# One core, column-normalised attention into a soft mixture of experts: first unit in one load, eight products of ones, 23 slots, half of turned v on VectorE, a new order

## Chip, cores and metric

One core of one Trainium2 chip. The metric is device time in microseconds (us). Before the change three runs took 286.63, 289.55 and 290.04 us, median 289.55 us.

## What is computed

B, N, C = 4, 5056, 256. All arrays are float32.

```
qn = q / (norm(q, axis=1) + 1e-6);  kn likewise          # norms over N, one per column
a  = softmax(kn.T @ qn / tau, axis=-1)                   # per batch, 256 x 256
x  = (v @ a).reshape(20224, 256)
logits = x @ phi                                         # 20224 x 32
d  = softmax(logits, axis=0);  slots = d.T @ x           # 8 experts x 4 slots x 256
out_e = relu(slots_e @ w1_e) @ w2_e                      # 256 -> 1024 -> 256
y  = softmax(logits, axis=1) @ out                       # 20224 x 256
```

q, k and v are read once (62 MB), v a second time in turned form for some of its parts (12.6 MB), the weights once (16.8 MB); 20.97 MB are written.

## The kernel before

**Stages.** q and k come in 40 units (ten per batch, 1 MB each: 128 partitions with 8 KB in a row; every unit has up to four tiles of 128 rows). For every tile TensorE adds kT q into one PSUM bank (`score`): straight from fp32 (L329, 4 instructions) or from a high and a low part (L335, 6 instructions), which ScalarE (`cast`, L274) and GpSimd (`low`, L278) make. ScalarE squares the unit (L289) and VectorE adds the squares (L307). After ten units the batch's norms, softmax and the product with phi follow (`att_...`), which give M, 256 x 32. v comes in 20 parts p (five per batch, 1 MB). The logits are M against v turned; for parts 2 to 13 the turned v is loaded (`load_vt`), for 0, 1 and 14 to 19 TensorE turns it (`turn`, L472, four 128 x 128 blocks into a bank) and ScalarE copies the bank to SBUF (`turned`, L477, 32 copies). `gather` (L601) then sums weighted v into slots. After the last part come the expert products (`up` L745, `relu`, `flip_h`, `back_h`, `down` L778, `o_copy`, `o_fold`, `o_back`) and the output (`out_mul` L816, `out_evict` L833, `store`), 40 blocks of softmax weights against the slots. The softmax over 32 slots (`c_max`, `c_sub`, `c_exp`, `c_sum`, `c_rec`, `c_mul`, `c_flip`) works on `nat`, 128 x 1280 per batch, mostly in VectorE passes.

**Order.** Nothing is scheduled by the compiler. `plan` lists some 1200 steps; `run` (L160) issues them in the sequence of the list `ORDER`, and every engine works through its own share of that sequence in order. All DMAs are issued by SyncE's queue (SP) in that order too: if one has to wait for its buffer, all behind it wait.

**Buffers.** All big tiles live in 22 slots of 8 KB per partition, named by `SLOTS`; a tile is written once the last reader of its slot's former tile is done. PSUM's eight banks are named by `BANKS` in the same way. The four `nat` tiles (5 KB each) and later the turned weights `cT` have places of their own.

**Start.** Unit 0 comes in three loads (L859: tile 0, tile 1, tiles 2 and 3). `constants` (identity, ones, an Exp to load ScalarE's table) stands behind the first products and squares. `wake` (L238) exists, but `WAKES` is empty.

Of the kernel before, what the change touches and what calls it, by code (L numbers as in the profile page):

```python
# [8 lines left out]
F32 = mybir.dt.float32  # L9
# [19 lines left out]
DVE_TURNED = set()  # L29

SAME = set()
WAKES = ()
# [62 lines left out]
]  # L95
SLOTS = {
# [70 lines left out]
def colnorm_attention_soft_moe(  # L167
# [22 lines left out]

    def slot(name, shape, dt=F32):
        return large.tile(shape, dt, tag=f"s{SLOTS[name]}", name=name)

    def bank(name):
        return ps.tile([P, 512], F32, tag=f"b{BANKS[name]}", name=name)

# [659 lines left out]
    for u in range(NU):  # L856
        b, i = divmod(u, UB)
        if u == 0:
            for lo, hi in ((0, 1), (1, 2), (2, 4)):  # L859
                at(-3, load_qk, 0, lo, hi)  # L860
# [204 lines left out]
```

## Time and profile before

| | |
|---|---|
| median of the runs | 289.55 us |
| the profiled execution | 288.49 us, its span 286.6 us |
| TensorE matmul, weight load busy | 250.2, 206.1 us |
| ScalarE, VectorE, GpSimd busy | 211.5, 200.7, 142.1 us |
| DMA | 112.90 MB, 394 GB/s over the span, queue share 96.7% |

The span is what the profiler saw of one execution from its first to its last event; the execution's own time is 1.9 us more. A share of busy time is a mean over stages: in the first 230 us all is read, in the last 55 us all is written, and GpSimd has work in the first 180 us only. A queue share near 100% means that bytes are moving nearly always.

### The profile page before, as it was taken

The numbers are of one execution on the slowest core, as the hardware profiler recorded it, in microseconds if no ns is written. First come the engines' busy times: TensorE is split into PE (matmuls) and PEld (weight loads), VectorE is DVE, ScalarE is ACT, GpSimd is POOL, SyncE is SP. The second block draws the span as 40 slices with busy tenths as digits, with TensorE's granted clock in tenths as the row PEclk, the third lists the DMA queues.
The fourth block names the chain that finished last, engine by engine and source line by source line (L and its number), as shares of the span: only waits on it lengthen the run. The fifth ranks groups of instructions, "written<-read, shape, count | busy, mean of one in ns | idle before, by whom it ended". The sixth has DMA issues, their size and how long they took to land.

```text
span 286.6 us, 6411 instructions
## 1 busy us (share of the span) xinstructions
PE 250.2 (87%) x2542; PEld 206.1 (72%) x2542; DVE 200.7 (70%) x386; ACT 211.5 (74%) x341; POOL 142.1 (50%) x118
## 2 busy tenths in 40 slices
PE   5799989999899998999999999999989899697300
PEld 3589879998699896787879779876643787595200
DVE  0156998778767679799579899589772487977600
ACT  3699999989989998989998978786633257446300
POOL 0379899798996998398899395100000000000000
PEclk9999999999999999999999999999989999959855
DMA  7999999999999999999999999999999959999996
GB/s 217 413 428 418 374 383 416 404 419 420 421 421 345 389 413 389 352 420 422 414 370 365 423 423 420 423 418 420 416 417 425 399 238 384 420 415 408 414 423 256
DMA packets 16301, 112.90 MB, mean 394 GB/s; under 512 B 1936, under 2 KB 1936, under 8 KB 3472
## 3 DMA queue, kind: packets, MB, share of 16 engines
q1 hardware_dynamic: 16272, 112.50, 96.7%
q8 instruction: 20, 0.33, 0.5%
q14 instruction: 9, 0.07, 0.1%
HBM read 91.52 MB, written 20.97 MB: 392 GB/s over the span
## 4 chain that ended last, share of the span: by engine, by line
PE 55%; DMA 23%; DVE 9%; ACT 4%; issue 2%; SPq 1%; DVEq 0%; ACTq 0%
PE S L335 19%; DMA v<-in_v_dram 10%; PE S L329 10%; DMA raw<-in_qk_dram 10%; PE op_None L816 4%; PE G L601 4%; DVE o L833 4%; PE T L472 3%; PE H L745 3%; PE O L778 3%; DMA x<-in_vt_dram 2%; DVE A L307 2%; PE L L492 2%; PE op L816 2%; PE Mp L425 1%
## 5 line engine op out<-in xcount | busy, mean ns | idle before, releaser
L278 POOL TENSOR_TENSOR hl<-raw,hl 128x512 fp32r<-128x512 f32 x108 | 137.5, 1312 | 33.5 <-ACT hl L274 27.0
L307 DVE TENSOR_TENSOR A<-sq,A 128x512 f32<-128x512 f32 (+1 forms) x144 | 95.2, 688 | 20.8 <-ACT sq L289 18.9
L335 PE MATMUL S<-hl 128*128 128x256 f32 x648 | 94.8, 295 | 0.0
L335 PEld LDWEIGHTS S<-hl 128*128 128x128 f32 x648 | 83.3, 190 | 3.9 <-issue 2.3
L289 ACT ACTIVATE sq<-raw 128x2048 f32<-128x2048 f32 (+2 forms) x40 | 71.5, 1803 | 6.5 <-DMA raw<-in_qk_dram 4.0
L329 PE MATMUL S<-raw 128*128 128x256 f32 (+1 forms) x208 | 52.2, 396 | 8.1 <-DMA raw<-in_qk_dram 8.1
L274 ACT CAST hl<-raw 128x1024 fp32r<-128x1024 f32 (+1 forms) x69 | 56.3, 863 | 3.1 <-DMA raw<-in_qk_dram 3.1
L329 PEld LDWEIGHTS S<-raw 128*128 128x128 f32 (+1 forms) x208 | 36.3, 195 | 15.5 <-DMA raw<-in_qk_dram 10.7
L816 PE MATMUL op_None<-so,cT 32*128 32x256 f32 x240 | 22.3, 436 | 3.4 <-DVE cT L720 2.7
L833 DVE COPY o<-op_None 128x512 f32<-128x512 f32 x30 | 18.9, 681 | 7.1 <-PE op_None L816 5.7
L833 ACT COPY o<-op_None 128x512 f32<-128x512 f32 x30 | 15.9, 591 | 9.2 <-PE op_None L816 9.1
L816 PEld LDWEIGHTS op_None<-so,cT 32*128 32x128 f32 x240 | 17.0, 204 | 7.7 <-DVE cT L720 3.5
L492 PE MATMUL L<-x,M 128*32 128x256 f32 (+1 forms) x320 | 20.6, 379 | 0.6 <-DMA x<-in_vt_dram 0.6
L601 PE MATMUL G<-v,dn 128*32 128x256 f32 x312 | 19.8, 381 | 1.3 <-DMA v<-in_v_dram 1.3
L477 ACT COPY x<-T 128x512 f32<-128x512 f32 x32 | 17.6, 602 | 2.3 <-PE T L472 2.3
L472 PE MATMUL T<-ident,v 128*128 128x128 f32 x124 | 16.8, 274 | 1.0 <-DMA v<-in_v_dram 0.9
L601 PEld LDWEIGHTS G<-v,dn 128*32 128x32 f32 x312 | 10.4, 109 | 7.3 <-DMA v<-in_v_dram 2.1
L472 PEld LDWEIGHTS T<-ident,v 128*128 128x128 f32 x124 | 14.0, 142 | 2.0 <-issue 0.8
L492 PEld LDWEIGHTS L<-x,M 128*32 128x32 f32 x320 | 10.3, 109 | 6.7 <-DVE cs L700 1.0
L816 PE MATMUL op<-so,cT 32*128 32x128 f32 x160 | 11.1, 324 | 2.8 <-ACT o L833 1.5
L816 PEld LDWEIGHTS op<-so,cT 32*128 32x128 f32 x160 | 9.3, 205 | 4.4 <-ACT o L833 1.9
L833 ACT COPY oh<-op 128x256 f32<-128x256 f32 x20 | 6.4, 381 | 6.8 <-PE op L816 6.7
(115 smaller groups left out, 247.8 us busy)
## 6 DMA issues: line engine op xcount, KB each, us to landing
raw<-in_qk_dram SPq DMA_DIRECT2D x37, 1024.0 KB, 8.9
v<-in_v_dram SPq DMA_DIRECT2D x16, 1024.0 KB, 9.3
w<-in_moe_w_dram SPq DMA_DIRECT2D x16, 1024.0 KB, 19.6
out_dram<-o SPq DMA_DIRECT2D x15, 1024.0 KB, 9.2
x<-in_vt_dram SPq DMA_DIRECT2D x12, 1024.0 KB, 7.8
out_dram<-oh SPq DMA_DIRECT2D x4, 1024.0 KB, 6.4
v<-in_v_dram SPq DMA_DIRECT2D x4, 896.0 KB, 10.3
raw<-in_qk_dram SPq DMA_DIRECT2D x2, 768.0 KB, 8.3
```

What stands on the lines that cost most here:

```text
L274: act.copy(parts(u, lo, hi)[:, :, 0::2, :], raws[u][:, lo:hi])
L278: pool.tensor_tensor(hl[:, :, 1::2, :], raws[u][:, lo:hi], hl[:, :, 0::2, :].bitcast(F32), op=ALU.subtract)
L289: act.activation(sqs[u][:, n : NT[u]], raws[u][:, n : NT[u]], AF.Square)
L307: dve.tensor_tensor(a[r], s[r, j], a[r], op=ALU.add)
L329: pe.matmul(sm, raw[r, j, 1, cols], raw[r, j, 0, :], start=first, stop=False, skip_group_check=True)
L335: pe.matmul(sm, hl[:, w, cols], hl[:, y, :], start=first, stop=False, skip_group_check=True)
L472: pe.transpose(tp[:, P * jj : P * jj + P], vtile(p, 4 * h + jj)[:, P * m : P * m + P], ident)
L477: to(xt(p)[:, m, h * UT : h * UT + UT], tps[p, h, m])
L492: pe.matmul(L[S * g : S * g + S, :n, :], M[:, m, :], x[:, :n, S * g : S * g + S], start=m == 0 and g not in void, stop=m == 1, skip_group_ ...
L601: pe.matmul(gp[S * g : S * g + S, :C], dn[:, x, j, :], vtile(p, j), start=x == 0 and j < G, stop=x == n - 1 and j >= G,)
L816: pe.matmul(ops[b, p, hf, g][:, h, :], cT[b][r, 4 * i : 4 * i + 4, :].rearrange("s j t -> s (j t)"), rhs[r], start=True, stop=True,)
L833: (dve.tensor_copy if g % 2 else act.copy)(dst, ops[b, p, hf, g])
```

## The change

- Unit 0 comes in one load (0 to 4).
- `WAKES = ((-8, 8),)`: eight products of `ones` by `ones` (128 x 128) ahead of all scores. `constants` moves to the front of every engine's list.
- `DVE_TURNED` names (p, h, 1) for all 20 parts: of the 32 copies of turned v, the 16 with m = 1 go to VectorE.
- 23 slots (0 to 22). The room comes from `nat`: only `nat0` and `nat1` keep places of their own, `nat2` and `nat3` take a slot each when their batch's first logits are ready; `cT3` takes the place of `nat2`.
- `ORDER`, `SLOTS` and `BANKS` are new throughout.

The diff without the three lists:

```
-DVE_TURNED = set()
+DVE_TURNED = {(9, 1, 1), (16, 0, 1), (10, 1, 1), (4, 0, 1), ...}
-WAKES = ()
+WAKES = ((-8, 8),)
+    def short(name):
+        t = slot(name, [P, 2 * C, 4]).rearrange("p c x -> p (c x)")
+        return t[:, : 8 * PB * S].rearrange("p (j s) -> p j s", s=S)
-    nat = [keep.tile([P, 8 * PB, S], F32, tag=f"nat{b}", name=f"nat{b}") for b in range(B)]
+    nat = [keep.tile([P, 8 * PB, S], F32, tag=f"nat{b}", name=f"nat{b}") for b in range(2)] + [None, None]
     def logit_nat(p):
         b, q = divmod(p, PB)
+        if nat[b] is None:
+            nat[b] = short(f"nat{b}")
     def c_flip(b, p):
         if b not in cT:
             if b == 0:
-                cT[b] = slot("cT0", [P, 2 * C, 4]).rearrange("p c x -> p (c x)")[:, : 8 * PB * S].rearrange(
-                    "p (j s) -> p j s", s=S
-                )
+                cT[b] = short("cT0")
+            elif b == 3:
+                cT[b] = nat[b - 1]
-            for lo, hi in ((0, 1), (1, 2), (2, 4)):
-                at(-3, load_qk, 0, lo, hi)
+            at(-3, load_qk, 0, 0, 4)
```

The new lists as the DMA queue sees them (q: unit of q and k, v: part of v, t: turned part, a: w1, b: w2, s: store of batch and part), before and after:

```
q0 q0 q0 q2 q4 q3 q1 q6 q5 q8 q7 q9 q10 q13 q11 q12 few v0 q14 q16 q15 q20 t3 v1 q19 t2 vh q17 t4 q21 q18 q23
q27 q26 q22 q25 v6 q24 v2 q35 q28 v3 t6 v4 q29 t5 q32 t7 q33 q30 q31 q34 t9 t8 q36 v9 q37 v5 v7 t10 v8 q38 t11
t12 q39 t13 v17 v14 v16 v15 v18 v12 v19 v10 v11 a1 v13 a3 a5 b01 a7 a6 a4 a2 a0 b00 b03 b02 b11 b10 b13 b12
s04.0 s01.0 s03.0 s10 s11 s14 s04.1 s20 s13 s12 s03.1 s24 s01.1 s32 s33 s30 s21 s31 s23 s34 s22

q0 q5 q6 q1 q3 q4 q9 q2 q7 q10 q8 q15 q11 q14 q12 v0 q13 q17 q16 v1 q19 q18 few t3 t2 q23 t4 q22 q20 q21 q37
q27 q24 q28 q29 q26 v2 q25 q31 t5 v4 vh t7 t6 q34 q30 t8 v3 t9 q32 q33 v6 v14 q35 q38 v5 t10 q36 t11 t13 v7
t12 v8 v9 q39 v16 v15 v17 v19 a1 a3 v18 v11 b00 v10 v12 v13 a0 a5 a2 a4 a7 a6 b03 b01 b02 b10 b11 b13 b12
s01.0 s03.0 s04.0 s11 s14 s12 s10 s01.1 s20 s03.1 s24 s13 s22 s32 s31 s30 s23 s04.1 s34 s33 s21
```

Other places that the prediction speaks of. In the old order ScalarE has `c_exp(2)` between the last part's exponentials and the sums that follow them (`tally`); in the new one it stands behind `last_back`, right ahead of `relu`. In the new order VectorE's `c_max(2)`, `c_sub(2)`, `c_mul(1)` and six of the `c_flip` steps of batches 0 and 1 stand behind `last_back` instead of ahead of it. Behind `o_copy(0)` VectorE's new list goes: `c_max(3)`, two `c_flip`, four copies of batch 0's first two output blocks, store.

## Rows read from the trace of the kernel before

**Rows 1.** Busy time by stretch (the window in us and its length, then busy time and instructions of PE, PEld, DVE, ACT and POOL, the granted TensorE clock, the DMA share, GB/s).

```profile
0.00:8.00 8.00, 3.78 (x8) 2.52 (x8) 0.00 (x0) 2.44 (x3) 0.20 (x4) 1.00 0.72 226
8.00:20.00 12.00, 10.58 (x54) 8.77 (x55) 5.09 (x18) 10.16 (x9) 5.96 (x7) 1.00 1.01 427
20.00:160.00 140.00, 135.62 (x1160) 119.30 (x1163) 111.23 (x200) 131.28 (x176) 121.28 (x97) 1.00 0.99 398
160.00:184.00 24.00, 23.14 (x230) 19.75 (x223) 22.98 (x43) 20.15 (x39) 14.61 (x11) 1.00 1.01 421
184.00:212.00 28.00, 27.13 (x364) 19.25 (x368) 19.61 (x50) 19.44 (x57) 0.00 (x0) 1.00 1.01 419
212.00:228.00 16.00, 15.07 (x214) 7.95 (x207) 7.41 (x11) 4.30 (x9) 0.00 (x0) 0.89 1.01 420
228.00:240.00 12.00, 11.26 (x271) 10.16 (x273) 8.65 (x21) 6.61 (x18) 0.00 (x0) 1.00 0.71 285
240.00:286.60 46.60, 23.64 (x266) 18.39 (x259) 25.69 (x46) 17.08 (x37) 0.00 (x0) 0.75 0.95 391
```

**Rows 2.** What the DMA queue's issues waited for between 20 and 160 us (total us, times, longest).

```profile
SPq L252 <- PE S L335: 24.8, 11, 4.6
SPq L467 <- PE S L335: 24.2, 7, 5.7
SPq L448 <- PE S L335: 11.3, 5, 3.5
SPq L252 <- ACT sq L289: 9.0, 3, 4.7
```

**Rows 3.** Pieces of the chain that ended last, in order of time (start, length, what; x counts instructions): the loads and products of the scores, of turned v, the last v load and the last stages.

```profile
13.41 1.99 PE S L329 x8
15.40 1.43 PE S L335 x12
...
20.23 0.86 PE S L329 x4
...
37.33 7.05 DMA v<-in_v_dram
...
47.95 0.44 PE T L472 x4
...
184.02 2.37 PE T L472 x20
...
188.27 1.73 PE G L601 x32
...
199.80 0.86 PE L L492 x16
...
207.64 1.17 ACT nat L696
...
211.88 8.74 PE H L745 x64
...
221.39 1.60 PE hTp L763 x12
223.00 3.67 PE O L778 x128
...
227.89 3.02 PE op L816 x61
```

**Rows 4.** TensorE's first instructions in order of time (start, busy time, what, count, idle before).

```profile
3.50 3.78 PE L329 MATMUL S<-raw 128*128 128x256 f32 x8 [3.50 <-DMA raw<-in_qk_dram]
8.43 1.99 PE L329 MATMUL S<-raw 128*128 128x256 f32 x8 [1.14 <-DMA raw<-in_qk_dram]
10.92 1.99 PE L329 MATMUL S<-raw 128*128 128x256 f32 x8 [0.50 <-DMA raw<-in_qk_dram]
```

**Rows 5.** The DMA queue's issues in order of time: the first loads and the first stores.

```profile
0.74 7.99 SPq L252 DMA_DIRECT2D raw<-in_qk_dram  x11
...
231.60 0.35 SPq L842 DMA_DIRECT2D out_dram<-oh  x1
```

**Rows 6.** The copies out of PSUM and VectorE's passes over `nat` (line, engine, operation, tiles, count, busy us, mean ns).

```profile
L477 ACT COPY x<-T 128x512 f32<-128x512 f32 x32 | 17.6, 602 | 2.3 <-PE T L472 2.3
L833 DVE COPY o<-op_None 128x512 f32<-128x512 f32 x30 | 18.9, 681 | 7.1 <-PE op_None L816 5.7 <-issue 1.4
L693 DVE TENSOR_TENSOR nat<-nat,cm 128x1280 f32<-128x1280 f32 x4 | 5.9, 1476 | 0.0
L720 DVE STREAM_TRANSPOSE cT<-nat 128x256 f32<-128x256 f32 x20 | 8.1, 424 | 0.2
```

More of the change, by code (lines that the diff above doesn't have):

```diff
@@ L28 @@
 LT = {2, 3, 4, 5, 6, 7, 8, 9, 10, 11, 12, 13}
-DVE_TURNED = set()
+DVE_TURNED = {(9, 1, 1), (16, 0, 1), (10, 1, 1), (4, 0, 1), (5, 0, 1), (11, 1, 1), (17, 1, 1), (15, 0, 1), (18, 0, 1), (0, 0, 1), (12, 0, 1), (1, 0, 1), (7, 1, 1), (13, 1, 1), (19, 1, 1), (2, 0, 1), (8, 0, 1), (14, 0, 1), (6, 1, 1), (3, 1, 1), (9, 0, 1), (15, 1, 1), (10, 0, 1), (16, 1, 1), (4, 1, 1), (11, 0, 1), (5, 1, 1), (6, 0, 1), (18, 1, 1), (0, 1, 1), (12, 1, 1), (2, 1, 1), (17, 0, 1), (7, 0, 1), (19, 0, 1), (8, 1, 1), (14, 1, 1), (3, 0, 1), (1, 1, 1), (13, 0, 1)}
 SAME = set()
-WAKES = ()
+WAKES = ((-8, 8),)
 ORDER = [
[59 rows of a table removed]
[59 rows of a table added]
 ]
 SLOTS = {
[25 rows of a table removed]
[25 rows of a table added]
 }
 BANKS = {
[33 rows of a table removed]
[33 rows of a table added]
 }
```

234 rows, old and new, of tables (BANKS, ORDER, SLOTS) are left out of this document.

## The prediction

> **What bounds the kernel now.** I read the busy time by stretch first. From 8 to 20 us and from 160 to 228 us bytes flow at 419 to 427 GB/s; I take 424 as the full stream. Three stretches fall short: the first 8 us, 20 to 160 us (398) and 228 to 240 us (285), where the loads are done and the stores have not begun [rows 1]. The waits of the DMA queue say why the middle is short: between 20 and 160 us its issues sat waiting for products that read a buffer's old content, 24.8, 24.2 and 11.3 us in the three largest groups [rows 2]. So the loads wait for slots, and TensorE for loads: the chain passes to and fro between products of the scores and loads, to v's last turned part, ready at 184.02 us [rows 3]. TensorE is busy 135.6 of 140 us there, ScalarE 131.3 [rows 1]: the room is small on every engine, and the DMA has the most.
>
> From 184 us on the chain is TensorE's and its neighbours': H at 211.88, the first output product at 227.89 [rows 3], the first store at 231.60 [rows 5]. From that store to the end are 55.0 us, of which 20.97 MB at 424 GB/s make 49.5. So **the end is the first store plus the stores**, and the first store hangs on TensorE's pace.
>
> **A count that ties it together.** I add up TensorE's work along its list with the chain's paces: 4 instructions of L329 0.86 us, 6 of L335 0.715, a turned block of four 0.44, logits 1.07 for a full part, gather 0.93 on average [rows 3]. The first product of v's last turned part stands behind 169.2 us of work, H behind 195.8. It ran at 184.02, H at 211.88: TensorE had lost 14.8 us by the one and 16.1 by the other. Of the 14.8, the start has 8.5: at 15.40 us [rows 3] only 32 instructions of L329, 6.9 us at pace, were done. The other 6.3 fell in the middle.
>
> **The start.** Before, 1.81 MB moved in the first 8 us [rows 1]; from 2 us on at full rate it would be 2.54, so 1.7 us of the stream are lost while the three small loads run. TensorE gets unit 0 in three lots, at 3.50, 8.43, and its next unit at 10.92 [rows 4]. After, unit 0 lands whole: the 256 KB issued at 0.74 [rows 5] landed by 3.50 [rows 4], 2.76 us; 0.79 MB more cost 1.85; so 5.3 us. TensorE then has 3.5 us of work, the next unit is there at 7.8, and so on each 2.47 us, while a unit of two split tiles is 3.2 us of TensorE's work: it need not wait again. Lost: 5.5 instead of 8.5, a gain of 3.0.
>
> The Trainium skill, "DMA: Bandwidth & Descriptors", section "Anatomy of one DMA", speaks against the one load: a fixed 2.0 us and bytes at 436 GB/s a DMA, for those that GpSimd issues. By it, as an estimate, the first product starts at 5.1 us instead of 3.3, and the trace's 3.50 agrees; what it says of the first product alone makes the change 1.8 us worse at that place, and it leaves out that the products behind it waited to 10.92.
>
> The first eight products took 3.78 us, the next eight 1.99 [rows 4], though the granted clock reads 1.00, which is 2.4 GHz, from the start [rows 1]. The eight products of ones stand in the wait for unit 0, so they cost nothing: sixteen instructions of half the columns are 1.7 us at pace and 3.8 at the slow one, and they only need `ones`, so they end at about 5 us. If they did nothing, unit 0 would cost 1.8 us more; if they ended late, some 1 us. I take zero; with the bounds the gain is 1.0 to 3.0. `constants` ahead of it all runs while every engine waits.
>
> **The slots.** For each load I compare its place in the stream (2 us plus all bytes up to it at 424 GB/s) with TensorE's work at the step that last reads its slot's old tile. The load of v's part 0 shows what that means: place 39.2, last reader a score behind 29.2 us of work, lead 10.0. It was issued at 37.33, 8.1 after its count, the loss so far, and landed 7.05 later [rows 3]; the bytes dip from there. A load is on time if its lead is over what TensorE has lost, less what the stream has lost, plus the way from issue to landing, 4.6 us (2.76 + 1.85). Late in the loop that is 14.8 - 8.2 + 4.6 = 11.2, with 8.2 for a stream whose v part 19, at place 170.9, came at 184.02 and needs some 5 of it for the start and its landing. The 51 loads between 15 and 68 MB have a mean lead of **11.5 us before** (least 6.3): half of them are late. In the new lists the mean is **16.0** (least 10.9; 16.3 over those whose reader is a product). A slot is worth 2.5 us; the rest is the order. With a loss of 5.5 to 9 the need is 10 to 12, so nearly all loads are on time.
>
> Nor does TensorE then run short: with landings at 5.3 us plus the bytes behind unit 0, the tightest loads land 4.5 us (unit 4), 3.8 (unit 18) and 2.2 (v's part 18) after the sum of the work ahead of them, all under the 5.5 that TensorE has lost already. The two w1 loads now ahead of v's part 18 make no wait.
>
> So the 6.3 us of the middle could go. I keep 3.5 of them: ScalarE has only 8.7 of the 140 us free [rows 1], and a middle that is 6.3 shorter would leave it 2.4, less than an engine that works strictly in order can use. H then starts at 195.8 + 5.5 + 3.5 + 1.3 (as before behind v's last part) = 206.1, **a gain of 5.8**; bounds 1.0 and 9.3.
>
> **The copies of turned v.** 16 times 602 ns leave ScalarE, 16 times about 681 come to VectorE, taking its 128 x 512 copy of the output [rows 6]. Twelve belong to parts 14 to 19: 8.2 us for VectorE where it was busy 23.0 of 24 and 19.6 of 28 us [rows 1]. What leaves that stretch: two subtractions or maxima and a product over `nat`, three times 1.47, and six turns of 0.42 [rows 6], 6.9 us, into the stretch of H, where VectorE had 7.4 of 16 [rows 1]. I cost it at zero, since those passes cover it; without that cover it costs up to 7.2 (8.2 less the idle 1.0).
>
> **The end.** `c_exp(2)` leaves ScalarE's chain to H, 1.17 us [rows 3], but VectorE's new list puts its passes there and the first sums still come last; zero to 1.2, I take 0. From H to the first output product 16.0 us before; after, 8.74 + 1.60 + 3.67 + four copies and a fold of 0.3 to 0.5 give 15.4 [rows 3]. VectorE, with c_max(3) of 1.47 and two turns ahead of four copies of 0.4, lets the first store go at H + 18.5, before at H + 19.7. The second store waits for a pass and four more copies, 1.3 us of stream. Gain 0 to 2, I take 0.7. The two `nat` tiles in slots cost late loads some lead, but w1 and w2 lead by 14 and more.
>
> **Sum.** 5.8 + 0.7 = 6.5: a span of 280.1; the execution's 288.49 becomes 282.0, and the median, 1.06 us above it, 283.0. I say **282.5 us**, 6.5 below 289.0, midway between the two. The loads then end at about 5.3 + 90.5 MB / 0.424 = 218.7, plus 1 to 3, the first store goes at 224.6: the hole between them gets wider than the 12 us stretch shows now.
>
> **Rivals.**
>
> *Only the start and the end pay.* The leads are sums of work without waits; if waits among ScalarE, VectorE and GpSimd fill the middle again, all 6.3 stay: 289.0 - 3.0 - 0.7 = 285.3, and with a start worth 1.0, 287. For it: ScalarE's and TensorE's busy time of 94 and 97% [rows 1]. Against it: the largest waits were the queue's [rows 2]. That the 23rd slot does nothing belongs here, since two slots are given up again to `nat`: then order alone must carry the lead.
>
> *VectorE becomes the bound* (the slower side). If parts 14 to 19 arrive in the old spacing, its 8.2 us of copies stand in a stretch that has 1.0 us free, its turned blocks come up to 7.2 us late, and logits, H and stores with them. It decides once VectorE holds over 24 us of work in the 24 us before v's last part. With the start's gain kept that is 289.0 - 3.0 + 7.2 = 293.2; with the middle's waits grown by as much as the start gained, 296. Against it: the 6.9 us moved out.
>
> *A full gain.* The middle's loss goes wholly and the end pays 2: 289.0 - 3.0 - 6.3 - 2.0 = 277.7. The stream allows it: 218.7 for the loads.
>
> **Numbers.** The forecast with the full gain, 277 to 284.5: 0.56. Start and end only, 284.5 to 289: 0.34. VectorE, up to 296: 0.10. A measurement can tell about 2%, 5.8 us, from no change: faster needs 283.8 or less. Forecast cases below it are 0.53; same 0.40; slower, above 295.3 or from several waits at once, 0.07. The range 277.5 to 289.0 leaves out one tenth above and a little below; the forecast's own is 277.5 to 284.5.
>
> **What would show it.** In the changed profile: the first products of L329 at 5 to 5.5 us, at 0.22 us each and with no gap till 15 us; the stream at 415 GB/s or more between 20 and 160 us; the queue's waits on L335 still long but harmless; v's part 18 before TensorE asks for it; H near 206; the first store near 225, behind a hole of 3 to 6 us; VectorE nearly full between 205 and 225. Wrong would be: 398 GB/s again in the middle (the leads), TensorE waiting for VectorE's turned copies (the second rival), or H at 206 and an end above 283 (stores that starve).

## The result

The changed kernel takes **280.03 us** (median of four runs, 279.50 to 280.23), the kernel before 288.09 us beside it: a ratio of 0.971, 95% interval 0.964 to 0.979, so faster. The same kernel again, in the last group of runs (e9 below), took 279.60 us, a ratio of 0.9705 (0.966 to 0.975) to the kernel before beside it. Executions more than 1.5% above the fastest of their kernel are left out of the ratios here and below, not out of the medians, and the profiled execution of e1 is one of them. The profiled execution took 280.23 us, its span is 278.4 us; before 288.49 and 286.6.

Busy time by stretch, in the stretches and columns of [rows 1]:

```profile
0.00:8.00 8.00, 5.68 (x26) 5.25 (x27) 1.31 (x13) 3.58 (x5) 0.70 (x6) 1.00 0.77 294
...
20.00:160.00 140.00, 139.62 (x1209) 122.78 (x1211) 121.22 (x217) 129.66 (x174) 118.41 (x96) 1.00 1.01 419
160.00:184.00 24.00, 24.00 (x233) 20.87 (x226) 22.17 (x46) 17.18 (x38) 13.56 (x10) 1.00 1.01 420
184.00:212.00 28.00, 27.69 (x351) 16.01 (x354) 20.74 (x46) 14.28 (x43) 0.00 (x0) 0.94 1.02 420
212.00:228.00 16.00, 14.69 (x352) 12.17 (x344) 12.26 (x26) 6.66 (x15) 0.00 (x0) 1.00 0.81 332
```

The stream between 20 and 160 us went from 398 to 419 GB/s, within 2% of the stretches beside it (426 and 420), and TensorE from 135.62 to 139.62 us busy. The hole between loads and stores moved for the most part from the 228 to 240 us stretch into the one before it. What the DMA queue waited for between 20 and 160 us:

```profile
SPq L452 <- PE S L339: 17.9, 6, 7.1
SPq L256 <- DVE A L311: 15.6, 6, 4.3
SPq L256 <- PE S L339: 15.0, 7, 7.3
```

Long waits again, as in [rows 2], but with 419 GB/s beside them they cost the stream nothing. **A wait in a queue is no loss by itself; the GB/s beside it tells.** The chain that ended last, and TensorE's first instructions:

```profile
0.74 4.99 DMA raw<-in_qk_dram
5.77 5.45 PE S L333 x24
...
42.15 0.62 ACT hl L278
...
42.82 5.05 POOL hl L282 x4
...
204.56 8.70 PE H L751 x64
213.26 1.98 PE hTp L769 x16
215.25 3.67 PE O L784 x128
...
220.14 1.65 PE op L822 x34
```
```profile
1.05 3.45 PE L245 MATMUL wake<-ones 128*128 128x128 f32 x16 [1.05 <-DVE ones L230]
5.77 5.45 PE L333 MATMUL S<-raw 128*128 128x256 f32 x24 [1.27 <-DMA raw<-in_qk_dram]
```

DMA has 2% of the chain, all of it unit 0's load (23% before). That is one execution: in e9, the same kernel, the chain runs through ScalarE and a load up to 37 us, DMA has 8%, and H starts at the same time, so the two paths are level there. Between 48 us and H the only pieces of note that are not TensorE's are ScalarE's sums (`tally`) from 199 us on. H starts at 204.56, 7.3 us earlier than in [rows 3]. The copies of turned v, and the first stores:

```profile
L481 DVE COPY x<-T 128x512 f32<-128x512 f32 x16 | 10.6, 679 | 1.3 <-PE T L476 1.1
...
L481 ACT COPY x<-T 128x512 f32<-128x512 f32 x16 | 8.9, 587 | 2.5 <-PE T L476 2.4
```
```profile
222.83 3.72 SPq L845 DMA_DIRECT2D out_dram<-oh  x2
229.66 0.33 SPq L848 DMA_DIRECT2D out_dram<-oh  x1
```

The first store goes 8.8 us earlier than in [rows 5], the end comes 8.2 us earlier.

### The profile page after: what moved, and what is told of

Its sections match the earlier page's. It is cut to its first block, busy times and chain, and to the rows that moved or that the text cites. A ratio compares the mean times of both kernels' runs of the same rounds, so it can differ in the third digit from the quotient of the medians.

```text
span 278.4 us, 6456 instructions
## 1 busy us (share of the span) xinstructions
PE 251.8 (90%) x2558; PEld 209.1 (75%) x2558; DVE 211.0 (76%) x402; ACT 203.5 (73%) x325; POOL 141.4 (51%) x118
## 4 chain that ended last, share of the span: by engine, by line
PE 82%; DVE 5%; ACT 2%; POOL 2%; DMA 2%; issue 1%; DVEq 0%; ACTq 0%
PE S L339 27%; PE S L333 16%; PE L L496 6%; PE G L607 6%; PE op_None L822 5%; PE T L476 5%; PE H L751 3%; PE O L784 3%; DVE o L839 2%; POOL hl L282 2%; DMA raw<-in_qk_dram 2%; PE op L822 2%; PE nn L352 1%; PE Mp L429 1%; PE cp L563 1%; DVE oh L839 1%
## 5 line engine op out<-in xcount | busy, mean ns | idle before, releaser
L311 DVE TENSOR_TENSOR A<-sq,A 128x512 f32<-128x512 f32 x144 | 94.5, 689 | 22.0 <-ACT sq L293 19.9
L339 PE MATMUL S<-hl 128*128 128x256 f32 x648 | 95.4, 295 | 0.4 <-POOL hl L282 0.2
L339 PEld LDWEIGHTS S<-hl 128*128 128x128 f32 x648 | 83.4, 190 | 3.6 <-POOL hl L282 0.8
L293 ACT ACTIVATE sq<-raw 128x2048 f32<-128x2048 f32 (+2 forms) x40 | 71.7, 1804 | 4.0 <-DVE A L311 1.9
L278 ACT CAST hl<-raw 128x512 fp32r<-128x512 f32 (+1 forms) x69 | 56.1, 857 | 1.2 <-PE S L339 0.7
L333 PE MATMUL S<-raw 128*128 128x256 f32 (+1 forms) x208 | 50.9, 384 | 1.3 <-DMA raw<-in_qk_dram 1.3
L496 PE MATMUL L<-x,M 128*32 128x256 f32 (+1 forms) x320 | 18.7, 378 | 0.0
L822 PE MATMUL op_None<-so,cT 32*128 32x256 f32 x160 | 15.3, 399 | 0.7 <-ACT o L839 0.3
L607 PEld LDWEIGHTS G<-v,dn 128*32 128x32 f32 x312 | 11.1, 109 | 5.1 <-issue 0.3
L822 PEld LDWEIGHTS op_None<-so,cT 32*128 32x128 f32 x160 | 11.4, 184 | 3.2 <-ACT o L839 1.8
L481 DVE COPY x<-T 128x512 f32<-128x512 f32 x16 | 10.6, 679 | 1.3 <-PE T L476 1.1
L481 ACT COPY x<-T 128x512 f32<-128x512 f32 x16 | 8.9, 587 | 2.5 <-PE T L476 2.4
## 6 DMA issues: line engine op xcount, KB each, us to landing
v<-in_v_dram SPq DMA_DIRECT2D x4, 896.0 KB, 11.5
```

What stands on the lines that cost most here:

```text
L278: act.copy(parts(u, lo, hi)[:, :, 0::2, :], raws[u][:, lo:hi])
L293: act.activation(sqs[u][:, n : NT[u]], raws[u][:, n : NT[u]], AF.Square)
L311: dve.tensor_tensor(a[r], s[r, j], a[r], op=ALU.add)
L333: pe.matmul(sm, raw[r, j, 1, cols], raw[r, j, 0, :], start=first, stop=False, skip_group_check=True)
L339: pe.matmul(sm, hl[:, w, cols], hl[:, y, :], start=first, stop=False, skip_group_check=True)
L481: to(xt(p)[:, m, h * UT : h * UT + UT], tps[p, h, m])
```

## The experiments

Twelve runs in three groups (e1 to e4, e5 to e8, e9 to e12, each group on a chip of its own), each with the kernel before beside it. Ratios are to that. The changed kernel itself ran beside the third group only (e9); where e3 to e8 are compared with its 280.03 us, the two come from different chips. "H" is the start of the first H product in the profiled execution, "stream" its GB/s between 20 and 160 us; e1 is judged by its times alone.

| run | edit | median us | ratio (95%) | H | stream |
|---|---|---|---|---|---|
| e1 | before + new start | 286.20 | 0.9945 (0.991 to 0.998) | | |
| e2 | before + 23 slots | 287.58 | 0.9988 (0.995 to 1.003) | 209.9 | 404 |
| e3 | changed, short load leads | 286.97 | 0.9991 (0.996 to 1.003) | 209.5 | 400 |
| e4 | changed, 22 slots | 289.61 | 1.0073 (1.004 to 1.011) | 213.2 | 405 |
| e5 | changed, tight engine tiles | 295.93 | 1.0283 (1.020 to 1.036) | 220.2 | 386 |
| e6 | changed, unit 0 in three loads | 282.04 | 0.9818 (0.976 to 0.987) | 205.9 | 419 |
| e7 | changed, no products of ones | 281.09 | 0.9772 (0.972 to 0.983) | 204.6 | 420 |
| e8 | changed, turned v on ScalarE | 284.36 | 0.9893 (0.985 to 0.993) | 208.6 | 419 |
| e9 | changed, no edit | 279.60 | 0.9705 (0.966 to 0.975) | 204.5 | 419 |
| e10 | changed, passes moved | 280.70 | 0.9735 (0.969 to 0.978) | 204.2 | 419 |
| e11 | changed, evened table | 283.54 | 0.9830 (0.979 to 0.987) | 208.0 | 410 |
| e12 | e10 and e11 | 284.10 | 0.9850 (0.980 to 0.990) | 208.2 | 409 |

### Single parts in the kernel before

e1, the start:

```diff
+        if u == 0:
+            if lo:
+                return
+            hi = 4
...
+        wake(8, 0)
...
-    for x in ORDER:
+    for x in [0] + [x for x in ORDER if x]:
```

> The kernel before, its order and its 22 slots, with the new start alone: unit 0 in one load, the constants first and the eight products of ones behind them. Theory (each part pays by its own; the leads of the slots set the middle): the start gives 1 to 3 us less than before, and of that the middle may take back some, since TensorE asks for the slots sooner only by what the loads already had; 285.5 to 288 where before is 288. The DMA stays near 400 GB/s between 20 and 160 us. Rival A (the start was nearly all of it): 280 to 282. Rival B (the order of before was laid out for small loads at the start, so the gain is lost at once): no change or slower, 288 to 290.

Measured: 0.55% less, 1.6 us, between 0.5 and 2.6. The theory holds; in the old order the start is worth about a fifth of the change, by the interval at most a third.

e2, the 23rd slot (the changes to `nat` are those of the kernel's own diff; `SLOTS` is handed out anew):

```diff
+    def short(name):
...
+    "hl1": 4, "sq2": 5, "raw6": 13, "hl2": 15, "sq3": 10, "raw7": 19, "hl3": 8, "sq4": 7, "raw8": 18, "hl4":
...
```

> The kernel before with its own order and start, but 23 slots of 8 KB; the last two of the four nat tiles stand in slots, and all slots are given out anew by the program's order of reads. The mean lead of the 51 middle loads is 12.3 us in place of 11.5, the least 8.6 in place of 6.3. Theory (lead sets the middle, and most of the lead came from the order, not from the slot): 1 to 2 us less than before, some 405 GB/s between 20 and 160 us. Rival (the 23rd slot is the change's core): 5 us less than before or more, 415 GB/s.

Measured: 0.12% less, with zero in the interval, though the profiled execution has H 1.9 us earlier. (The profiled executions of e2 and e3 lie 0.9 and 1.4 us below their medians, so their H is early for their time.) In the old order the slot buys next to nothing, less than even the theory said. So neither part that can be carried over alone makes the gain; it comes with the order, and the next runs ask what in the order.

### The same order with other tables of slots

e3 keeps every engine's order and only hands out the 23 slots differently, so that loads follow close on their slot's old tile (one line of the table as an example):

```diff
-    "raw11": 13, "hl7": 12, "sq8": 11, "raw12": 18, "hl8": 18, "v1": 12, "sq9": 2, "raw13": 15, "hl9": 10,
...
+    14, "hl7": 9, "sq8": 11, "raw12": 13, "hl8": 18, "v1": 13, "sq9": 2, "raw13": 9, "hl9": 10, "sq10": 13,
```

> The changed kernel with only its table of slots replaced: the same order on every engine, the same start, the same 23 slots, but handed out so that loads follow closely on the last reader of the slot's old tile: mean lead 12.0 us (16.0 in the changed kernel, 11.5 before), least 7.0, 23 of 51 loads under 10 (none, and 14 before). Theory (lead decides the middle): the stalls of the middle come back, 4 to 7 us slower than the changed kernel, 284 to 287, the stream at 400 to 408 GB/s between 20 and 160 us, TensorE waiting for loads there again. Rival (the new order of the engines did it by itself, leads or not): within 1 us of the changed kernel.

Measured: 286.97, 7 us slower than the changed kernel and level with the one before, the stream back at 400 GB/s. **The gain of the order is gone when the leads are gone.** Counted on e3's own lists, the tiles that the engines write, which the next runs are about, are no tighter than in the changed kernel (one of them, `hl23`, has under half a microsecond of TensorE's work between the old tile's last reader and itself, in both kernels). e4 gives the new order 22 slots:

```diff
-    nat = [keep.tile([P, 8 * PB, S], F32, tag=f"nat{b}", name=f"nat{b}") for b in range(2)] + [None, None]
+    nat = [keep.tile([P, 8 * PB, S], F32, tag=f"nat{b}", name=f"nat{b}") for b in range(B)]
...
```

> The changed kernel with 22 slots, the last two nat tiles in places of their own as before, and the slots given out again for the longest leads: mean lead 14.7 us, least 10.1; three entries of the list moved by one or two places so that it can be laid out. Theory (leads over the need of 10 to 12 us cost nothing, so the order and the hand-out of slots did it, not the number of slots): 0 to 1.5 us slower than the changed kernel. Rival (the 23rd slot itself carries the gain): 4 us slower or more.

Measured: 289.61, 9.6 us slower, slower even than the kernel before. My theory failed: the loads' leads were long (mean 14.7) and the time was lost all the same. The costliest groups of the page tell where: ScalarE's squares (L293), its casts (L278) and TensorE's products from the split parts (L339). The last columns are the idle time before them and what ended most of it. The changed kernel, then e3, then e4:

```profile
L339 PE MATMUL S<-hl 128*128 128x256 f32 x648 | 95.4, 295 | 0.4 <-POOL hl L282 0.2
...
L293 ACT ACTIVATE sq<-raw 128x2048 f32<-128x2048 f32 (+2 forms) x40 | 71.7, 1804 | 4.0 <-DVE A L311 1.9
L278 ACT CAST hl<-raw 128x512 fp32r<-128x512 f32 (+1 forms) x69 | 56.1, 857 | 1.2 <-PE S L339 0.7
```
```profile
L293 ACT ACTIVATE sq<-raw 128x2048 f32<-128x2048 f32 (+2 forms) x40 | 71.7, 1807 | 5.4 <-DMA raw<-in_qk_dram 4.7
L278 ACT CAST hl<-raw 128x512 fp32r<-128x512 f32 (+1 forms) x69 | 56.4, 860 | 4.4 <-DMA raw<-in_qk_dram 4.4
```
```profile
L339 PE MATMUL S<-hl 128*128 128x256 f32 x648 | 96.3, 295 | 3.0 <-POOL hl L282 2.8
...
L293 ACT ACTIVATE sq<-raw 128x2048 f32<-128x2048 f32 (+2 forms) x40 | 71.6, 1803 | 10.2 <-PE S L339 4.4
L278 ACT CAST hl<-raw 128x512 fp32r<-128x512 f32 (+1 forms) x69 | 56.0, 856 | 5.1 <-PE G L607 3.0
```

In e3 ScalarE waits for data to come (DMA, 9.1 of the 9.8 us): late loads. In e4 the largest part of its wait, 8.2 of 15.3 us, ends with a product of TensorE (PE S, PE G, PE L), which lets go of a place to write to, and 2.2 us end with a load, as in the changed kernel (2.1): **the tiles that ScalarE and GpSimd write need a lead as well.** Squares and split operands live in the same slots. In e4 seven of the 80 such tiles had less than half a microsecond of TensorE's work between the old tile's last reader and themselves, in the changed kernel one. e5 tests that with 23 slots, no moved entry, and longer load leads than the changed kernel has:

```diff
-    "x12": 7, "hl46": 1, "nat2": 21, "raw38": 4, "sq35": 10, "hl47": 16, "raw39": 2, "hl48": 11, "v13": 19,
...
+    20, "hl46": 16, "nat2": 14, "raw38": 6, "sq35": 10, "hl47": 15, "raw39": 17, "hl48": 13, "v13": 21,
```

> The changed kernel with only its table of slots replaced; order, start and 23 slots stay. The loads keep their leads (mean 16.5 us, least 11.7; 16.0 and 11.0 in the changed kernel), but the tiles that ScalarE and GpSimd write (squares, split operands) get slots whose old tile is read until just before: 5 of the 80 have under half a microsecond of TensorE's work between the old tile's last reader and their own first writer (1 in the changed kernel, 7 in the new order with 22 slots), and 28 under 3 us (17 and 22). New theory, formed on the run with 22 slots (tiles written by ScalarE need a lead as loads do, and the 23rd slot gives it): 3 to 8 us slower than the changed kernel, with ScalarE waiting for products on the squares' line. Rival (loads' leads alone decide, and the run with 22 slots lost its time by its three moved entries or its least lead of 10.1): within 1 us of the changed kernel.

Measured: 295.93, 16 us slower, twice what I had said at most. The rival is out. The same three groups in e5:

```profile
L339 PE MATMUL S<-hl 128*128 128x256 f32 x648 | 97.1, 296 | 5.0 <-POOL hl L282 4.9
...
L293 ACT ACTIVATE sq<-raw 128x2048 f32<-128x2048 f32 (+2 forms) x40 | 71.8, 1805 | 13.1 <-PE S L333 4.4
L278 ACT CAST hl<-raw 128x512 fp32r<-128x512 f32 (+1 forms) x69 | 56.3, 856 | 8.8 <-PE S L339 4.2
```

ScalarE idles 21.9 us before its two big jobs, in the changed kernel 5.2: 16.7 us more, and H is 15.7 us later. Of the 21.9 us 13.2 end with a product of TensorE and 0.4 with a load. No other engine of e5 waits for a load between 8 and 221 us, so late loads, the other way to lose this time, are out as well. TensorE now waits 4.9 us for the split operands, which wait for the casts, which wait for TensorE's products; and as all engines fall behind, the stream falls to 386 GB/s with leads that were longer than in the changed kernel.

The Trainium skill, "Perfetto Trace Analysis", section "Optimization Strategy", says that a gap that repeats on the engine that should be full can mean too little SBUF for the next tile. The traces of e4 and e5 agree (3.0 and 5.0 us of gaps before TensorE's products from split parts, 0.4 in the changed kernel), with one addition: e5 has as many slots as the changed kernel, so there it was not their number but who got which.

e11 goes the other way and takes lead from loads to give it to the engines' tiles:

```diff
-    "hl1": 21, "sq2": 20, "raw6": 5, "hl2": 12, "sq3": 13, "raw7": 22, "hl3": 15, "sq4": 16, "raw8": 8,
...
+    "hl1": 7, "sq2": 22, "raw6": 1, "hl2": 18, "sq3": 11, "raw7": 11, "hl3": 4, "sq4": 8, "raw8": 21, "hl4":
```

> The changed kernel with only its table of slots replaced, by one that trades load leads for leads of the engines' tiles: loads mean 14.6 us, least 9.2, 3 under 11 (16.0, 11.0 and 1 in the changed kernel); of the 80 tiles of ScalarE and GpSimd 7 have under 3 us of TensorE's work (17). Theory (both kinds of lead are already enough in the changed kernel, where the stream runs at 419 GB/s and ScalarE waits little for old tiles): within 1 us. Rival A (the 17 tight tiles still cost time): 1 to 3 us faster, H earlier. Rival B (leads near 10 already stall loads): 1 to 3 us slower, the stream under 415 GB/s in the middle.

Measured: 3.9 us slower than e9 beside it; rival B's side, and more than it said. What the queue waited for between 10 and 32 us, and the stretch from 22 to 24 us, in e11:

```profile
SPq L256 <- DVE A L311: 22.2, 2, 17.7
```
```profile
22.00:24.00 2.00, 2.00 (x13) 1.85 (x12) 1.97 (x4) 0.90 (x1) 2.00 (x3) 1.00 0.50 86
```

One load, `raw7`, shares slot 11 with the squares `sq3` there and waits 17.7 us until VectorE has added them up; all loads behind it wait too, and for 2 us the DMA moves 86 GB/s. My lead counted TensorE's work up to that place in the list; VectorE came to it later. A lead by TensorE's list is a measure for slots that TensorE reads last, and flatters the others. How much of the 3.9 us is this one entry, and how much the leads near 10, was not tried apart. All of it is lost ahead of 110 us: against e9, batch 0's product with phi is 2.6 us late (72.32 for 69.71), batch 1's 3.5 (110.12 for 106.63), and H 3.5. Unit 0's products also ran slowly in this execution (24 in 7.79 us for 5.45), which may be part of it.

### The start in the changed kernel

e6 brings the three loads back, e7 leaves the products of ones out:

```diff
-        sp.dma_start(raws[u][:, lo:hi], src[:, lo:hi])
+        for a, z in ((0, 1), (1, 2), (2, 4)) if u == 0 else ((lo, hi),):
+            sp.dma_start(raws[u][:, a:z], src[:, a:z])
```

> The changed kernel with unit 0 in three loads again, 256, 256 and 512 KB; the products of ones stay. Theory (TensorE's first work in one piece saves the waits between the lots, as computed before: 5.5 us lost in place of 8.5): 1.5 to 3 us slower than the changed kernel; the first product is ready at 3.5 us, yet TensorE has lost 7 us or more at 15 us. Rival (the earlier first lot pays for the smaller loads): no change, within 0.7 us.

```diff
     def wake(k, n):
+        return
```

> The changed kernel without the eight products of ones; they feed no result. Theory (they stand in the wait for unit 0 and make unit 0's products run at 0.22 us from the first): the first eight products take 3.5 to 3.8 us in place of 1.8, TensorE is 1.8 us later, and the end by 1 to 2 us. Rival A (the pace comes with time from the program's start, not with TensorE's own work): no change, first products at 0.22 us. Rival B (slots absorb a late TensorE, so the end stays): first products slow, time within 0.5 us.

Measured: e6 2.0 us slower than the changed kernel, as expected, but its first product starts at 4.63 us, behind the products of ones, and not at 3.5; e7 1.1 us slower by the medians, but its profiled execution, the second fastest of six, has the same H (204.6) and nearly the same span (278.1; e9, whose H ran at the full clock as e7's did, 277.8). The count of score products that TensorE had begun by 15, 35 and 80 us (window, busy time and count, granted clock, DMA share, GB/s), in the changed kernel, e7 and e6:

```profile
0.00:15.00 15.00, 9.23 (x51) 1.00 0.88 357
0.00:35.00 35.00, 29.23 (x177) 1.00 0.96 393
0.00:80.00 80.00, 65.92 (x414) 1.00 0.99 408
```
```profile
0.00:15.00 15.00, 9.35 (x39) 1.00 0.88 357
0.00:35.00 35.00, 29.35 (x166) 1.00 0.96 394
0.00:80.00 80.00, 66.62 (x413) 1.00 0.99 408
```
```profile
0.00:15.00 15.00, 8.26 (x32) 0.89 0.86 322
...
0.00:80.00 80.00, 65.78 (x406) 0.98 0.99 402
```

Without the products of ones TensorE is 12 products behind at 15 us, 11 at 35 and one at 80; with three loads it is 19 behind at 15 us and 8 at 80. How unit 0's products ran in e7, and the piece of e6's chain in which they stand:

```profile
5.65 7.05 PE L334 MATMUL S<-raw 128*128 128x256 f32 x24 [5.65 <-DMA raw<-in_qk_dram]
```
```profile
7.82 6.27 PE S L334 x20
```

TensorE is done with unit 0 at 11.22 us in the changed kernel, at 12.70 in e7 and at 14.09 in e6, so 1.5 and 2.9 us later. From batch 1's product with phi (106.62, 106.69 and 108.07 us) to H it is 0.1 and 1.4 us later. In both, 1.4 us have been absorbed on the way: there the changed kernel waits for what the others make, as in the chain at 42 us. The rest reaches H whole. e6's stream is behind too, 402 against 408 GB/s over 80 us, but from 7.82 us to the last sums before H no load stands in e6's chain, only TensorE. **About 1.4 us of TensorE's late start cost the changed kernel nothing; what goes beyond reaches H.** For e7, rival B is right about the profiled execution; whether the median's 1.1 us is real is open.

### The copies of turned v

```diff
-DVE_TURNED = {(9, 1, 1), (16, 0, 1), (10, 1, 1), (4, 0, 1), ...}
+DVE_TURNED = set()
```

> The changed kernel with all 32 copies of turned v by ScalarE again, in the new order. Theory (VectorE took 16 of them at no cost because passes were moved out, and ScalarE had 8.7 us free in 140): within 1.5 us of the changed kernel, to the slower side, since ScalarE gets 9.6 us more and was the fuller engine. Rival A (ScalarE's relief is what made the middle shorter): 4 us slower or more, ScalarE waited for between 100 and 184 us. Rival B (VectorE is the bound late, so that giving the copies back helps): 1 us faster or more.

Measured: 284.36, 4.3 us slower: rival A's size, but not its place. H is 4.1 us later, and the stretch from 20 to 160 us shows no loss:

```profile
20.00:160.00 140.00, 139.98 (x1200) 123.77 (x1202) 117.17 (x208) 131.27 (x179) 118.24 (x96) 1.00 1.01 419
```

Against the changed kernel, batch 1's product with phi is 0.8 us late (107.46 for 106.62) and batch 2's still 0.8 (155.06 for 154.22); the last batch's is 2.3 late (186.18 for 183.91) and the gather behind it 3.7 (193.77 for 190.09). So 3.3 of the 4.1 us arise behind 160 us, where v's last parts are turned; the 0.8 are there from the first 70 us on, in an execution whose unit 0 was done at 13.06 us for 11.22. From the chain that ended last in e8:

```profile
182.55 1.94 ACT x L481 x4
...
187.73 0.59 ACT x L481
188.32 0.36 ACT M L441 x2
188.68 1.45 ACT x L481 x3
```

ScalarE's copies stand on the path there, one behind the other. In the changed kernel the trace names nobody who waits for a copy of turned v.

### The end

e10 moves three steps (1005, 1006 and 1007 in the list: `c_max(3)`, `c_sub(3)`, `c_exp(3)`):

```diff
-    1005, 1033, 1034, 1054, 971, 1055, 990, 1059, 1000, 1056, 1058, 1057, 1063, 1060, 1061, 970, 1062, 1065,
-    1066, 1068, 1004, 1006, 1070, 1071, 1039, 1040, 1041, 1069, 1007, 1074, 1064, 1002, 1042, 1047, 1048,
...
+    1032, 1033, 1034, 1054, 971, 1055, 990, 1059, 1000, 1056, 1058, 1057, 1063, 1060, 1061, 970, 1062, 1065,
...
+    1050, 1073, 1067, 1005, 1006, 1001, 1075, 1051, 1007, 1052, 1053, 1076, 1077, 1078, 1080, 1079, 1081,
```

> The changed kernel with three steps of the list moved: c_max(3) and c_sub(3), 1.48 and 1.45 us of VectorE, go behind the first sixteen copies of the output, and c_exp(3) behind them on ScalarE. Theory (between the loads' end and the stores the path is TensorE, and it waits for banks that these copies empty): the second half of O starts 1 us earlier, the first store up to 1.5 us earlier, the end 1 us earlier, 279. Rival A (the passes stand in VectorE's idle time): no change. Rival B (the passes now delay o_copy(1), the next sums): 0.5 to 1 us slower.

e9 is the bar beside it, without an edit:

> The changed kernel itself, unaltered, as the bar for the three beside it: every theory expects 280, within half a per cent of it, and 0.97 of the kernel before.

Measured: 280.70 against 279.60 in e9, rival B's direction, though the two intervals overlap. VectorE in e10, then in e9:

```profile
223.50 1.47 DVE L696 TENSOR_REDUCE cm<-nat 128x40 f32<-128x1280 f32 x1
225.00 1.49 DVE L699 TENSOR_TENSOR nat<-nat,cm 128x1280 f32<-128x1280 f32 x1
226.41 0.44 DVE L726 STREAM_TRANSPOSE cT<-nat 128x256 f32<-128x256 f32 x1
226.77 0.25 DVE L796 COPY ob<-O 128x128 f32<-128x128 f32 x1
```
```profile
226.57 0.29 DVE L796 COPY ob<-O 128x128 f32<-128x128 f32 x1 [0.74 <-PE O L784]
```

The second half of O starts 0.75 us earlier in e10 (222.06 for 222.81). But 0.3 of that was there at H (204.17 for 204.49), ahead of the moved steps, as at unit 0's first product (5.53 for 5.76); the move gave 0.4. And `o_copy(1)` no longer waits for O: it stands behind the passes and starts 0.2 us later than in e9. The gain is eaten at the next step of the same engine: from H to the end are 74.0 us in e10 and 73.3 in e9.

e12 has both edits:

> The moved passes and the evened table together. Theory: the sum of the two runs beside it, that is 1 us under the changed kernel from the passes and nothing from the table; 279. Rival (the two gains sit on the same wait): no more than the better of the two.

Measured: 284.10, e11 and nothing off. No version beats the changed kernel.

## Why the prediction was right

Forecast 282.5 us, measured 280.03: faster, inside the range and in the forecast's own case. The bound and the way to lift it were right; several sizes were not, and some of them cancelled. Step by step:

- **Bound and mechanism.** Right, as far as it went. Late loads set the middle; with longer leads the stream is full (419 GB/s, above the 415 named) and H comes early. e3 takes the leads alone away and the gain goes. H at 204.56 for 206.1 is most of what the time lies below the forecast: span 278.4 for 280.1.
- **The start.** Unit 0 landed 0.4 us later than the 5.3 worked out: first product at 5.77, outside the 5 to 5.5 named; 0.227 us each, no gap. That TensorE's 3.0 us all reach H was wrong: with three loads TensorE is 2.9 us later behind unit 0, and 1.4 of them reach H (e6); in the old order the start gives 1.6 us of time (e1). Both are within the bounds of 1.0 to 3.0. The products of ones were put at zero cost, and at 1.8 us if they did nothing; TensorE does lose 1.6 us without them (24 products in 7.05 us for 5.45), but H loses nothing.
- **What the middle keeps.** 3.5 us was too much: TensorE lost 8.8 at H (204.56 less the 195.8 of work), 5.8 of it at the start; with 1.3 behind v's last part, as assumed and not measured, 1.7 are left for the middle, little more than the 1.4 that a late start gets for nothing. The reason given was that ScalarE would be left with too little idle time, 2.4 of the 140 us. The runs do not bear it out: ScalarE has 10.3 us free there now, and in e8, with all 32 copies back on it, 8.7 as before, while TensorE is busy 139.98 us at 419 GB/s. The start was put 0.3 us too low and the middle 1.8 too high.
- **"A slot is worth 2.5 us; the rest is the order."** This was said of the lead. By the leads on record a slot gave 0.8 us in the old order (11.5 to 12.3, e2) and 1.3 in the new (14.7 to 16.0, e4). In time neither part stands alone: the slot by itself gives nothing (e2), and without it the new order is worse than the old (e4). The sum of leads looked at loads alone. What runs short in e4 is the room for ScalarE's and GpSimd's tiles, which the prediction never counted; that the changed kernel's table leaves this room was luck as far as the prediction goes.
- **Turned copies on VectorE at zero.** Right for VectorE: with them it is busy 22.17 of the 24 us from 160 on, 22.98 before [rows 1], and nobody waits for its copies of turned v. The rival of a bound VectorE fell with that. The other side of the move was left out: what leaves ScalarE is worth 3.3 us of H behind 160 us (e8), and the forecast put nothing there. Without it, in an order laid out for it, H is at 208.59, 2.5 us behind the 206.1 forecast, and the time 284.36: that the forecast came so near was in part luck.
- **The end.** Right. H to first store 18.3 us (18.5 forecast, 19.7 before), and of these 1.4 us 0.6 were given back behind it, where the next store waits till 229.66: 0.9 gained, 0.7 forecast. VectorE was less full than said, 16.9 of the 20 us from 205 to 225.
- **Start and end only.** e3 comes nearest to this rival, with start and end changed and the leads short: 287 us, its upper figure, and by the ratio no gain at all over the kernel before beside it (0.9991).

## What to carry to other kernels

Where one pool of buffers serves loads and engines, count for every tile how much work lies between its slot's last reader and its own writer, for the tiles that engines write as for loads, and on the list of the engine that reads last (one entry of e11 shows why). A wait in a DMA queue matters only where the bytes beside it fall. Ask what an engine idles for, data (e3) or room (e4, e5): with the same number of slots, a table can be long on the one and short on the other. A head start is worth only what later waits do not absorb: here 1.4 us of a late start were free and the rest reached H.

## What the runs showed that was not expected

- The products of ones do not always set the pace. In the changed kernel, e1, e3, e4, e9, e10 and e12 unit 0's products ran at 0.23 us behind them; in e5, e8 and e11 they started slowly all the same (24 in 7.87 us in e5, in 7.37 in e8, for 5.45). The granted clock reads 1.00, 2.4 GHz, throughout in all of these, so the records don't explain it. The Trainium skill, "TensorE: Matmul & The Clock Gate", section "Part 1: The HAM clock gate (the "warmup" mystery)", has the array's clock at 1.2 GHz by default and released by activity; the durations look like that, the granted clock here does not show it.
- In e6 it does show: after 2.11 us without a product the granted clock was 0.57 from 8 to 9 us and 0.50, 1.2 GHz, from 9 to 11, and 20 products took 6.27 us.
- In the changed kernel's profiled execution the granted clock was 0.50 from 206 to 208 us, in H, in e9 1.00. H took 8.70 us in the one and 7.07 in the other, but O began only 0.7 us apart (215.25 and 214.53): behind a fast H TensorE waits for ScalarE's `relu`, which stands behind the passes over `nat` and starts at 210.99 and 210.98. So at the full clock VectorE's passes are on the path to O after all.
